# Attention scores of the first batch from plain fp32 products instead of products of rounded parts

## The chip, the cores and the metric

The kernel runs on one core of a Trainium2 chip. The metric is device time in microseconds (us), from the first to the last instruction and what lies around them. The core has five engines that run their own instruction streams in order: TensorE (PE; its weight loads are PEld), VectorE (DVE), ScalarE (ACT), GpSimd (POOL) and SyncE (SP, which here only issues transfers). They wait for each other by semaphores.

## The reference

Three stages follow one another. The first is attention over 4 batches of 8 heads, 576 positions, 64 numbers a head, with a threshold on the scores:

```
scores = scale * np.matmul(q, k.transpose(0, 1, 3, 2))
thresh = np.max(scores, axis=-1, keepdims=True) - tau
scores = np.where(scores >= thresh, scores, -1000000000.0)
scores = scores - np.max(scores, axis=-1, keepdims=True)
attn = np.exp(scores)
attn = attn / (np.sum(attn, axis=-1, keepdims=True) + 1e-09)
return np.matmul(attn, v).astype(np.float32)
```

The second is a dense layer pair (2304 tokens, 512 to 2048 to 512, a leaky rectifier between), the third a mixture of 8 experts with one expert a token. Both the threshold and the choice of the expert are decided by comparisons, so the products before them have to be close to fp32.

## The kernel before

**How precision is kept.** Most products run on numbers rounded to the type fp32r: the kernel splits an operand into a rounded part and a rounded residue and adds up the products of the parts. For scores, q and k of a pair of heads arrive twice: on partitions 0 to 63 and again on 64 to 127. The tile `qs` gets q rounded on all 128 partitions (ScalarE, L118 and L124), and then on partitions 64 to 127 the residue (`sub`, L110, on VectorE for pair 0 and on GpSimd for the others). The tiles `khh` and `kll` hold k times the scale, rounded (ScalarE, L116 and L122), and its residue (VectorE, `sub_k`, L113). One product of `qs` and `khh` over 128 partitions is then (q rounded + q residue) times k rounded, and one of `qs` and `kll` adds the same times k's residue.

**How the work is tiled.** A pair of heads (16 pairs, four a batch) has nine tiles of 128 score rows, numbered t = 0 to 8; n counts tiles over all pairs, i = n // 9 is the pair. Tile t = 4 holds the last 64 rows of the first head and the first 64 of the second. A tile's scores are two column halves of 288, each the sum of two products (t = 4: four), so four instructions at L152 (t = 4: eight). Then: the row's minimum of the negated scores (VectorE, L160), a bias (L164), the exponential (ScalarE, L169), the mask with its row sum (VectorE, L177), the split of the result in two 16-bit parts (ScalarE L196, GpSimd L197), a transposition by DMA (SP, L201), and five tiles later the products with v (TensorE, L216 or L222 to L224), scaled on the way out (L247 to L253). In the first batch, six tiles of nine take 25 products with v of 64 columns (L216), two take 15 and t = 4 takes 30.

**What sets the order.** A string is gone through once a tile, and each letter issues one step:

```
ORD = "QSMVaCRBbKOPcrTLoXd"
```

Q issues the scores of tile n + 2, S the split of n - 1, M the maximum of n + 1, V the products with v of n - 5, C one step of converting the dense layer's weights (ScalarE, VectorE, GpSimd; L382 to L390), B the bias of n + 1, K the mask of n, P a step of the next pair's preparation, T the transposition of n - 1, L the loads of pair i + 2, X the exponential of n + 1. The products with v are written beside the scores of tile n + 2 in the same PSUM tile, of which there are three. So the scores of n + 2 wait for the mask of n - 1, and the maximum of n + 2 waits for the scores and for the products with v that were issued right after them.

The preparation of a pair (`prep`) is a generator: each P takes one step of it (two in pair 0). The raw tiles of q, k and v have one buffer each, so a load waits until the pair before has been split. `LAT` says at which t the loads of k, q and v are issued. From tile 36 on other work (a class `Units`) is put between the steps; up to there only the weight conversion is.

Of the kernel before, what the change touches and what calls it, by code (L numbers as in the profile page):

```python
# [11 lines left out]
F32 = mybir.dt.float32  # L12
F32R = mybir.dt.float32r
# [3 lines left out]
AF = mybir.ActivationFunctionType  # L17
# [6 lines left out]
P = 128  # L24
B, H, S, D = 4, 8, 576, 64
HP = H // 2
# [15 lines left out]
def f(ap):  # L42
    return ap.bitcast(F32)


class Attention:
    def __init__(self, tc, ctx, qkt, vt, tau, xd):
        self.tc, self.qkt, self.vt, self.xd = tc, qkt, vt, xd
        nc = tc.nc
        cp = ctx.enter_context(tc.tile_pool(name="a_const", bufs=1))  # L50
        self.ld = ctx.enter_context(tc.tile_pool(name="a_ld", bufs=1))
        self.sp = ctx.enter_context(tc.tile_pool(name="a_split", bufs=2))
        self.ep = ctx.enter_context(tc.tile_pool(name="a_e", bufs=2))
        self.sm = ctx.enter_context(tc.tile_pool(name="a_sm", bufs=8))
        self.ptp = ctx.enter_context(tc.tile_pool(name="a_pt", bufs=PVL + 1))
        self.ps_s = ctx.enter_context(tc.tile_pool(name="a_ps_s", bufs=3, space=PSUM))
        tt = cp.tile([P, 1], F32, name="tau")
        nc.sync.dma_start(tt, tau.to_broadcast([P, 1]))
        self.c2 = cp.tile([P, 2], F32, name="c2")
        nc.vector.memset(self.c2, LNC)  # L60
        first = cp.tile([P, 1], F32, name="first")
        nc.scalar.activation(first, self.c2[:, 1:2], AF.Exp)
        keep = cp.tile([P, 1], F32, name="keep")
        nc.vector.tensor_scalar(keep, tt, 0.0, None, op0=ALU.is_ge)
        self.qsc = cp.tile([P, 1], F32, name="qsc")
        nc.vector.tensor_scalar(self.qsc, keep, -1.0 / float(D) ** 0.5, None, op0=ALU.mult)
        c1 = cp.tile([P, 1], F32, name="c1")
        nc.vector.tensor_scalar(c1, tt, 0.0, None, op0=ALU.max)
        nc.vector.tensor_scalar(keep, keep, -1.0, 1.0, op0=ALU.mult, op1=ALU.add)
        nc.vector.tensor_tensor(self.c2[:, 0:1], c1, keep, op=ALU.add)  # L70

        self.qs_b = [cp.tile([P, 2, 640], F32R, name=f"qs{i}") for i in range(2)]
        self.p_b = [cp.tile([P, 2, 640], F16, name=f"p{i}") for i in range(NP)]
        self.ss_b = [cp.tile([P, 9, 2], F32, name=f"ss{i}") for i in range(3)]
        self.rs_b = [cp.tile([P, 9], F32, name=f"rs{i}") for i in range(3)]
        for t in self.ss_b:
            nc.gpsimd.memset(t, 1e-9 * math.exp(LNC))
        for t in self.qs_b:
            nc.gpsimd.memset(f(t[:, 0, S:640]), 0.0)
        for t in self.p_b:  # L80
            nc.gpsimd.memset(t[:, :, S:640], 0.0)

    def load(self, k, i):

        nc = self.tc.nc
        b, hp = divmod(i, HP)
        r = self.raws.setdefault(i, {})
        if k < 2:
            r[k] = self.ld.tile([P, 2, S], F32, tag="qk"[k], name="raw_qk")
            if i:  # L90
                nc.sync.dma_start(r[k], self.qkt[b, hp][:, k])
        else:
            r[k] = self.ld.tile([P, 2, 5, D], F32, tag="v", name="raw_v")
            if i == 0:
                for h, j in ((0, 1), (0, 0), (1, 1), (1, 0)):
                    nc.sync.dma_start(r[j][:, h], self.qkt[b, hp][:, j, h])
            nc.sync.dma_start(r[k], self.vt[b, hp])

    def prep(self, i, eng):

        nc, sp, qsc = self.tc.nc, self.sp, self.qsc
        raw = self.raws.pop(i)
        qr, kr, vr = (raw[k] for k in range(3))
        qs = self.qs_b[i % 2]
        kk = [[sp.tile([P, S], F32R, tag=t, name=t, bufs=3) for t in ("khh", "kll")] for _ in range(2)]
        vs = sp.tile([P, 2, 5, 3, D], BF16, tag="vs", name="vs")
        vd = sp.tile([P, 2, 5, D], F32, tag="vd", name="vd", bufs=1)

        def sub(o, a, b, k):
            (eng if SUBS[k] == "p" else nc.vector).tensor_tensor(o, a, b, op=ALU.subtract)  # L110

        def sub_k(h):
            nc.vector.scalar_tensor_tensor(kk[h][1], kr[:, h], qsc, f(kk[h][0]), op0=ALU.mult, op1=ALU.subtract)  # L113

        self.pr[i] = qs, kk, vs
        nc.scalar.activation(kk[0][0], kr[:, 0], AF.Copy, scale=qsc)  # L116
        yield
        nc.scalar.activation(qs[:, 0, 0:S], qr[:, 0], AF.Copy)  # L118
        sub_k(0)
        yield  # L120
        sub(qs[D:P, 0, 0:S], qr[D:P, 0], f(qs[D:P, 0, 0:S]), 0)
        nc.scalar.activation(kk[1][0], kr[:, 1], AF.Copy, scale=qsc)  # L122
        yield
        nc.scalar.activation(qs[:, 1, 0:S], qr[:, 1], AF.Copy)  # L124
        sub_k(1)
        yield
        sub(qs[D:P, 1, 0:S], qr[D:P, 1], f(qs[D:P, 1, 0:S]), 1)
        yield
        nc.scalar.activation(vs[:, :, :, 0], vr, AF.Copy)
        yield  # L130
        sub(vd, vr, vs[:, :, :, 0], 2)
        yield
        nc.scalar.activation(vs[:, :, :, 1], vd, AF.Copy)
        yield
        sub(vs[:, :, :, 2], vd, vs[:, :, :, 1], 3)

    def score_mm(self, n):
        nc = self.tc.nc
# [124 lines left out]
    def run(self, npair):  # L263

        nc = self.tc.nc
# [14 lines left out]
        for n in range(nn + PVL + 2):  # L280
            i, t = divmod(n, 9)
            for w in ORD:
                if w == "a":
                    yield "start"
                elif w == "b":
                    yield "mid"
                elif w == "c":
                    yield "late"
                elif w == "C":
                    yield "conv"  # L290
                elif w == "d":
                    yield "tail"
                elif w == "P":
                    if t == 0 and i + 1 < npair:
                        g_prep = self.prep(i + 1, nc.gpsimd)
                        if i == 0:
                            g_prep = itertools.chain(g, [None] * 4, g_prep)
                    for _ in range(2 if i == 0 else 1):
                        next(g_prep, None)
                elif w == "S":  # L300
                    if 0 < n <= nn:
                        self.split(n - 1)
                elif w == "M":
                    if n + 1 < nn:
                        self.score_max(n + 1)
                elif w == "R":
                    if n <= nn:
                        self.sums(n - 1, 1)
                elif w == "O":
                    self.pv_out(1)  # L310
                elif w == "B":
                    if n + 1 < nn:
                        self.score_bias(n + 1)
                elif w == "Q":
                    if n + 2 < nn:
                        self.score_mm(n + 2)
                    else:
                        self.free = self.ps_s.tile([P, 2, 512], F32, tag="s", name="s")[:, 1, 320:320 + 2 * D]
                elif w == "V":
                    last, self.done = self.done, []  # L320
                    if 0 <= n - PVL < nn:
                        self.pv(n - PVL)
                elif w == "K":
                    if n < nn:
                        self.score_mask(n)
                elif w == "X":
                    if n + 1 < nn:
                        self.score_exp(n + 1)
                elif w == "T":
                    if 0 < n <= nn:  # L330
                        self.turn(n - 1)
                elif w == "o":
                    self.pv_out(0, last)
                elif w == "r":
                    if n < nn:
                        self.sums(n, 0)
                elif w == "L":
                    if n < 3:
                        self.load((1, 0, 2)[n], 1)
                    k = LAT[i > 0].find(str(t))  # L340
                    if k >= 0 and i + 2 < npair:
                        self.load((1, 0, 2)[k], i + 2)
            yield "end"


# [847 lines left out]
LAT = ["678", "457"]  # L1193
# [154 lines left out]
def body(tc, qkt, vt, tau, win, wout, mid, wg, wgt, mb, w1, w2, out):  # L1348
    nc = tc.nc
    with ExitStack() as top, tc.manual_schedule():  # L1350
# [12 lines left out]
        with ExitStack() as c1:  # L1363
            c0 = ExitStack()
            tp = c0.enter_context(tc.tile_pool(name="first", bufs=1, side="right"))
            at = Attention(tc, c1, qkt, vt, tau, xd)
            steps = at.run(B * HP)
            next(steps)
            cv = mo.convs(list(range(NF)), itertools.cycle(un.raws).__next__,
# [148 lines left out]
```

## Time and profile before

| | |
|---|---|
| three runs, us | 1058.48, 1061.03, 1061.22 (median 1061.03) |
| profiled execution, us | 1063.25, its span 1061.5 |
| mean granted clock of TensorE | 0.954 of full speed |
| busy over the span | TensorE 89%, VectorE 75%, ScalarE 56%, GpSimd 39% |

The page gives shares over the whole span; a stage is read from the views that can be cut to a stretch: busy time by stretch, groups of instructions by source line, waits, and the timeline. The clock column is the share of full speed that TensorE was granted: its levels are 1.2 GHz (0.5) and 2.4 GHz (1.0), so a mean between them says how much of a stretch was spent at which. In the first 28 us the column reads 1.00, while the score products start 0.24 us apart as they do at 1.2 GHz elsewhere; there the timeline is to be believed. The score tiles of the first batch are those between the first mask at 10.76 us and the 36th at about 113 us.

### The profile page before, as it was taken

Reading aid. Unit: us, or ns where it says so; the run is one execution under the profiler, and the core shown is the slowest. Engines: PE = TensorE matmul, PEld = TensorE weight load, DVE = VectorE, ACT = ScalarE, POOL = GpSimd, SP = SyncE. Lnnn points to the kernel's source line nnn. Section 1 sums busy time; section 2 is a strip of 40 time slices with the busy share of each in tenths; the row PEclk is TensorE's granted clock in tenths of the full one; section 3 lists DMA queues with packets and bytes.
Section 4 is the critical chain, followed back from the end, with each engine's and each line's share of the span. In section 5 each row is a group of like instructions: output and inputs, shape, how many; then the busy total and the mean of one; then the engine's idle time right before and its main releaser. Section 6 shows DMA issues by size and latency. Waiting matters only on the chain. (4 is left out here: it accounts for less than half of the span.)

```text
span 1061.5 us, 21618 instructions
## 1 busy us (share of the span) xinstructions
PE 944.1 (89%) x7593; PEld 841.5 (79%) x7593; DVE 790.8 (75%) x1975; ACT 597.7 (56%) x1234; POOL 415.0 (39%) x376
## 2 busy tenths in 40 slices
PE   4676679998999999788899999999989999999983
PEld 3666568888888999667788888989878999898962
DVE  7999988888888885887777777475558666655573
ACT  6677787888788875444222222323345555565473
POOL 3889887777778673332000000000102211121121
PEclk9879889999999999799999999999989999999997
DMA  8999999999999997542322321100555998665573
GB/s 216 197 223 222 232 243 228 211 218 254 210 196 242 236 181 144 177 143 84 112 61 60 60 41 41 41 21 1 120 180 153 341 300 289 229 242 169 171 253 118
DMA packets 278766, 182.03 MB, mean 171 GB/s; under 512 B 204450, under 2 KB 241446, under 8 KB 278632
## 3 DMA queue, kind: packets, MB, share of 16 engines
q1 hardware_dynamic: 270176, 165.25, 64.5%
q0 software_dynamic: 4736, 12.92, 3.6%
q10 hardware_dynamic: 3720, 2.22, 0.7%
q8 instruction: 65, 1.06, 0.5%
q14 instruction: 69, 0.57, 0.2%
HBM read 115.74 MB, written 18.22 MB: 126 GB/s over the span
## 5 line engine op out<-in xcount | busy, mean ns | idle before, releaser
L449 PE MATMUL y<-w,g 128*128 128x512 f32 x960 | 259.5, 406 | 0.0
L197 POOL TENSOR_TENSOR p<-p,p 128x576 f16<-128x576 f32 x144 | 193.1, 1342 | 86.9 <-ACT p L196 69.7
L449 PEld LDWEIGHTS y<-w,g 128*128 128x128 f32 x960 | 173.2, 193 | 29.6
L417 PE MATMUL h<-uxh,w 128*128 128x256 f32 x848 | 168.7, 295 | 17.4 <-POOL w L390 6.5
L417 PEld LDWEIGHTS h<-uxh,w 128*128 128x128 f32 x848 | 138.6, 195 | 31.0 <-DVE g L431 11.5
L152 PE MATMUL s<-khh,qs 128*128 128x288 f32 x320 | 107.2, 348 | 45.7 <-DVE p L177 23.0
L160 DVE TENSOR_REDUCE s<-s 128x1 f32<-128x576 f32 x144 | 109.3, 759 | 38.7 <-PE s L224 34.0
L429 ACT ACTIVATE g<-h 128x256 fp32r<-128x256 f32 x144 | 55.4, 385 | 129.3 <-DVE h L427 127.4
L417 PE MATMUL h<-uxl,w 128*128 128x256 f32 x424 | 122.3, 289 | 0.7 <-DVE uxl L408 0.7
L601 POOL DMA_INDIRECT idt<-ids,pi x18 | 18.7, 1040 | 264.2 <-DVE pi L598 196.4
L222 PE MATMUL s<-vs,pt 128*128 128x128 bf16 (+1 forms) x680 | 109.9, 229 | 13.6 <-DMA pt<-p 13.4
L177 DVE SCALAR_TENSOR_TENSOR p<-s,tb,e 128x576 f32<-128x576 f32 x144 | 117.0, 813 | 0.7 <-ACT e L169 0.6
L425 ACT ACTIVATE ct<-h 128x256 f32<-128x256 f32 x144 | 55.2, 383 | 109.9 <-PE h L417 102.7
L152 PEld LDWEIGHTS s<-khh,qs 128*128 128x128 f32 x320 | 67.8, 212 | 54.1 <-DVE p L177 15.5
L169 ACT ACTIVATE e<-s,tb 128x576 f32<-128x576 f32 x144 | 106.8, 741 | 4.9 <-DVE tb L164 4.9
L224 PE MATMUL s<-vs,pt 128*128 128x128 bf16 (+1 forms) x680 | 108.1, 226 | 0.0
L223 PE MATMUL s<-vs,pt 128*128 128x64 bf16 (+1 forms) x680 | 104.7, 198 | 0.0
L427 DVE SCALAR_TENSOR_TENSOR h<-h,ct 128x256 f32<-128x256 f32 x144 | 61.5, 427 | 54.5 <-ACT ct L425 53.8
L196 ACT ACTIVATE p<-p 128x576 f16<-128x576 f32 x144 | 99.2, 689 | 3.4 <-DVE p L177 2.1
L152 PE MATMUL s<-kll,qs 128*128 128x288 f32 x320 | 98.8, 322 | 0.0
L222 PEld LDWEIGHTS <-pt 128*128 128x128 f16 (+1 forms) x680 | 68.8, 104 | 26.4 <-DMA pt<-p 16.5
L417 PE MATMUL h<-exh,w 128*128 128x256 f32 (+1 forms) x448 | 85.8, 287 | 0.7 <-ACT exh L406 0.7
(233 smaller groups left out, 2270.2 us busy)
## 6 DMA issues: line engine op xcount, KB each, us to landing
cr<-w SPq DMA_DIRECT2D x36, 512.0 KB
raw_qk<-qkt SPq DMA_DIRECT2D x30, 576.0 KB
raw<-w SPq DMA_DIRECT2D x24, 512.0 KB
eraw<-w SPq DMA_DIRECT2D x18, 512.0 KB
cr<-w_in SPq DMA_DIRECT2D x16, 512.0 KB
cr<-w_out SPq DMA_DIRECT2D x16, 512.0 KB
ur<-xd SPq DMA_DIRECT2D x15, 512.0 KB
ur<-w SPq DMA_DIRECT2D x12, 512.0 KB
```

The lines of the kernel that those rows point to most:

```text
L152: nc.tensor.matmul(s[:, j, 0:288], qf[:, c0:c0 + P], x[:, j * 288:(j + 1) * 288], start=(k == 0), stop=(k == len(ops) - 1))
L160: v.tensor_reduce(self.mq[n], self.sq[n], axis=AX.XY, op=ALU.min)
L169: self.tc.nc.scalar.activation(e, self.sq[n], AF.Exp, bias=self.mq[n][:, 1:2], scale=-1.0)
L177: self.tc.nc.vector.scalar_tensor_tensor(p, self.sq.pop(n), self.mq.pop(n)[:, 0:1], self.eq.pop(n), op0=ALU.is_le, op1=ALU.mult, accum_out ...
L196: nc.scalar.activation(pp[:, 0, 0:S], p, AF.Copy)
L197: nc.gpsimd.tensor_tensor(pp[:, 1, 0:S], p, pp[:, 0, 0:S], op=ALU.subtract)
L222: nc.tensor.matmul(o[r0:r1, 0:2 * D], hi, v12, start=(c == 0), stop=False)
L223: nc.tensor.matmul(o[r0:r1, D:2 * D], hi, vs[:, h, c, 2], start=False, stop=False)
L224: nc.tensor.matmul(o[r0:r1, 0:2 * D], lo, v12, start=False, stop=(c == 4))
L417: nc.tensor.matmul(h, w[:, 0, a, s], b[:, c], start=(n == 0), stop=(n == 11))
L427: nc.vector.scalar_tensor_tensor(h, h, 0.01, a, op0=ALU.mult, op1=ALU.max)
L449: nc.tensor.matmul(y, a[:, s], w[:, 1, b], start=start and k == 0, stop=stop and k == 2)
```

## The change

For the four pairs of the first batch (i < HP) q and k are loaded once, on partitions 0 to 63. q goes to one of two new tiles `qa0` and `qa1` of its own and is used as it is; k is scaled by ScalarE into a `khh` tile seen as fp32. There are no residues of q and k. A tile's scores are one plain fp32 product for each column half (t = 4: two). The preparation of such a pair has seven steps instead of nine: v's four steps come two tiles earlier. The loads of pair 3 are issued at t = 4 (k) and 7 (q and v) of pair 1 instead of 4, 5 and 7. From pair 4 on everything is as it was; the old steps have moved into a function of their own, `prep_parts`.

```
@@ -44,7 +44,7 @@
 
 
 class Attention:
-    def __init__(self, tc, ctx, qkt, vt, tau, xd):
+    def __init__(self, tc, ctx, q0p, qkt, vt, tau, xd):
         self.tc, self.qkt, self.vt, self.xd = tc, qkt, vt, xd
         nc = tc.nc
         cp = ctx.enter_context(tc.tile_pool(name="a_const", bufs=1))
@@ -75,6 +75,9 @@
         self.rs_b = [cp.tile([P, 9], F32, name=f"rs{i}") for i in range(3)]
         for t in self.ss_b:
             nc.gpsimd.memset(t, 1e-9 * math.exp(LNC))
+        self.q0 = [q0p.tile([P, 2, 640], F32, name=f"qa{i}") for i in range(2)]
+        for t in self.q0:
+            nc.gpsimd.memset(t[0:D, 0, S:640], 0.0)
         for t in self.qs_b:
             nc.gpsimd.memset(f(t[:, 0, S:640]), 0.0)
         for t in self.p_b:
@@ -86,14 +89,19 @@
         b, hp = divmod(i, HP)
         r = self.raws.setdefault(i, {})
         if k < 2:
-            r[k] = self.ld.tile([P, 2, S], F32, tag="qk"[k], name="raw_qk")
+            if i < HP and k == 0:
+                r[k] = self.q0[i % 2][0:D, :, 0:S]
+            else:
+                r[k] = self.ld.tile([P, 2, S], F32, tag="qk"[k], name="raw_qk")
+                if i < HP:
+                    r[k] = r[k][0:D]
             if i:
-                nc.sync.dma_start(r[k], self.qkt[b, hp][:, k])
+                nc.sync.dma_start(r[k], self.qkt[b, hp][0:D if i < HP else P, k])
         else:
             r[k] = self.ld.tile([P, 2, 5, D], F32, tag="v", name="raw_v")
             if i == 0:
                 for h, j in ((0, 1), (0, 0), (1, 1), (1, 0)):
-                    nc.sync.dma_start(r[j][:, h], self.qkt[b, hp][:, j, h])
+                    nc.sync.dma_start(r[j][:, h], self.qkt[b, hp][0:D, j, h])
             nc.sync.dma_start(r[k], self.vt[b, hp])
 
     def prep(self, i, eng):
@@ -102,7 +110,11 @@
         raw = self.raws.pop(i)
         qr, kr, vr = (raw[k] for k in range(3))
         qs = self.qs_b[i % 2]
-        kk = [[sp.tile([P, S], F32R, tag=t, name=t, bufs=3) for t in ("khh", "kll")] for _ in range(2)]
+        if i < HP:
+            kk = [[f(sp.tile([P, S], F32R, tag="khh", name="khh", bufs=3))[0:D]] for _ in range(2)]
+            qs = self.q0[i % 2][0:D]
+        else:
+            kk = [[sp.tile([P, S], F32R, tag=t, name=t, bufs=3) for t in ("khh", "kll")] for _ in range(2)]
         vs = sp.tile([P, 2, 5, 3, D], BF16, tag="vs", name="vs")
         vd = sp.tile([P, 2, 5, D], F32, tag="vd", name="vd", bufs=1)
 
@@ -113,6 +125,24 @@
             nc.vector.scalar_tensor_tensor(kk[h][1], kr[:, h], qsc, f(kk[h][0]), op0=ALU.mult, op1=ALU.subtract)
 
         self.pr[i] = qs, kk, vs
+        if i < HP:
+            nc.scalar.activation(kk[0][0], kr[:, 0], AF.Copy, scale=qsc[0:D])
+            yield
+            yield
+            nc.scalar.activation(kk[1][0], kr[:, 1], AF.Copy, scale=qsc[0:D])
+            yield
+        else:
+            yield from self.prep_parts(qs, kk, qr, kr, sub, sub_k)
+        nc.scalar.activation(vs[:, :, :, 0], vr, AF.Copy)
+        yield
+        sub(vd, vr, vs[:, :, :, 0], 2)
+        yield
+        nc.scalar.activation(vs[:, :, :, 1], vd, AF.Copy)
+        yield
+        sub(vs[:, :, :, 2], vd, vs[:, :, :, 1], 3)
+
+    def prep_parts(self, qs, kk, qr, kr, sub, sub_k):
+        nc, qsc = self.tc.nc, self.qsc
...
@@ -337,9 +360,10 @@
                 elif w == "L":
                     if n < 3:
                         self.load((1, 0, 2)[n], 1)
-                    k = LAT[i > 0].find(str(t))
-                    if k >= 0 and i + 2 < npair:
-                        self.load((1, 0, 2)[k], i + 2)
+                    lat = "477" if 0 < i < HP - 2 else LAT[i > 0]
+                    for k in range(3):
+                        if lat[k] == str(t) and i + 2 < npair:
+                            self.load((1, 0, 2)[k], i + 2)
             yield "end"
 
 
@@ -1363,7 +1387,7 @@
         with ExitStack() as c1:
             c0 = ExitStack()
             tp = c0.enter_context(tc.tile_pool(name="first", bufs=1, side="right"))
-            at = Attention(tc, c1, qkt, vt, tau, xd)
+            at = Attention(tc, c1, tp, qkt, vt, tau, xd)
             steps = at.run(B * HP)
             next(steps)
             cv = mo.convs(list(range(NF)), itertools.cycle(un.raws).__next__,
```

In the program order of TensorE, at the start: before, the first two tiles of scores (`s_177`, `s_182`), from q's split tile `qs0` and the parts of k of the first head.

```order
L152 MATMUL s_177<-khh_166,qs0_131 128x288 [waits DVE_49]
L152 MATMUL s_177<-kll_167,qs0_131 128x288
L152 MATMUL s_177<-khh_166,qs0_131 128x288
L152 MATMUL s_177<-kll_167,qs0_131 128x288
L152 MATMUL s_182<-khh_166,qs0_131 128x288
L152 MATMUL s_182<-kll_167,qs0_131 128x288
L152 MATMUL s_182<-khh_166,qs0_131 128x288
L152 MATMUL s_182<-kll_167,qs0_131 128x288
```

Now the same place; `qa0` is q as loaded, `khh` the scaled k, and "x2" stands for two equal rows.

```order
L175 MATMUL s_175<-khh_169,qa0_148 128x288 [waits DMAHW2_49,Activation_49]
L175 MATMUL s_175<-khh_169,qa0_148 128x288
L175 MATMUL s_178<-khh_169,qa0_148 128x288 x2
L175 MATMUL s_186<-khh_169,qa0_148 128x288 x2
L175 MATMUL s_200<-khh_169,qa0_148 128x288 [waits DVE_49,PE_49]
L175 MATMUL s_200<-khh_169,qa0_148 128x288
```

Four products a tile have become two, and the first of them waits for a load (DMAHW) and ScalarE instead of VectorE. Later in the batch, VectorE's program order, from the mask of tile 5 (`p_351`) to the maximum of tile 8 (`s_362`), before:

```order
L177 SCALAR_TENSOR_TENSOR p_351,ss0_139<-s_270,tb_298,e_311 128x576 [waits Activation_49,Pool_49]
L113 SCALAR_TENSOR_TENSOR kll_303<-raw_qk_205,qsc_125,khh_302 128x576 [waits DMAHW0_49]
L187 TENSOR_REDUCE rs0_142<-ss0_139 128x3 [waits DVE_49]
L160 TENSOR_REDUCE s_313<-s_313 128x1 [waits PE_49]
L385 SCALAR_TENSOR_TENSOR yt1_92<-cr1_89,yt1_92 128x512
L189 RECIPROCAL rs0_142<-rs0_142 128x3 [waits DVE_49]
L164 TENSOR_TENSOR tb_387<-c2_119,s_313 128x2 [waits DVE_49]
L177 SCALAR_TENSOR_TENSOR p_389,ss0_139<-s_288,tb_349,e_360 128x576 [waits Activation_49,Pool_49]
L113 SCALAR_TENSOR_TENSOR kll_305<-raw_qk_205,qsc_125,khh_304 128x576
L160 TENSOR_REDUCE s_362<-s_362 128x1 [waits PE_49]
```

Now, from the mask of tile 5 (`p_326`) to the maximum of tile 8 (`s_335`); line numbers are those of the changed file, 23 or 24 higher.

```order
L200 SCALAR_TENSOR_TENSOR p_326,ss0_139<-s_252,tb_281,e_288 128x576 [waits Activation_49,Pool_49]
L210 TENSOR_REDUCE rs0_142<-ss0_139 128x3 [waits DVE_49]
L183 TENSOR_REDUCE s_290<-s_290 128x1 [waits PE_49]
L409 SCALAR_TENSOR_TENSOR yt1_92<-cr1_89,yt1_92 128x512
L212 RECIPROCAL rs0_142<-rs0_142 128x3 [waits DVE_49]
L187 TENSOR_TENSOR tb_358<-c2_119,s_290 128x2 [waits DVE_49]
L200 SCALAR_TENSOR_TENSOR p_360,ss0_139<-s_273,tb_324,e_333 128x576 [waits Activation_49,Pool_49]
L183 TENSOR_REDUCE s_335<-s_335 128x1 [waits PE_49]
```

The two residues of k (`kll`) behind the masks are gone; the steps of the weight conversion (`yt1`) and the sums (`rs0`) stand where they stood.

## Rows read from the trace of the kernel before

**Rows 1.** The page: busy time of the engines, and two of the 40 slices' rows.
```profile
PE 944.1 (89%) x7593; PEld 841.5 (79%) x7593; DVE 790.8 (75%) x1975; ACT 597.7 (56%) x1234; POOL 415.0 (39%) x376
...
PE   4676679998999999788899999999989999999983
...
DVE  7999988888888885887777777475558666655573
```

**Rows 2.** Busy time, clock and DMA by stretch; the line of columns is the second.
```profile
core 0: us, PE busy (x) PEld busy (x) DVE busy (x) ACT busy (x) POOL busy (x), PEclk, DMA share, GB/s
10.70:114.00 103.30, 69.28 (x849) 61.54 (x848) 99.15 (x215) 76.26 (x142) 83.81 (x71) 0.83 1.04 216
30.00:114.00 84.00, 57.73 (x780) 51.81 (x780) 79.95 (x174) 61.63 (x119) 72.16 (x64) 0.80 1.05 218
150.00:240.00 90.00, 83.27 (x897) 75.70 (x896) 77.09 (x211) 74.16 (x153) 68.55 (x60) 0.98 1.10 220
```

**Rows 3.** Groups by line, VectorE, 10.7 to 114 us: busy, mean ns, idle before.
```profile
L160 DVE TENSOR_REDUCE s<-s 128x1 f32<-128x576 f32 x35 | 26.4, 753 | 3.5 <-PE s L216 2.3 <-PE s L224 1.2
...
L113 DVE SCALAR_TENSOR_TENSOR kll<-raw_qk,qsc,khh 128x576 fp32r<-128x576 f32 x9 | 9.2, 1018 | 0.0
...
L110 DVE TENSOR_TENSOR qs<-raw_qk,qs 64x576 fp32r<-64x576 f32 x1 | 0.8, 755 | 0.0
```

**Rows 4.** Waits, 10.7 to 114 us: total us, times, longest.
```profile
PE s L152 <- DVE p L177: 21.9, 18, 2.9
...
PE s L222 <- DMA pt<-p: 0.8, 1, 0.8
```

**Rows 5.** Timeline, a cold tile: start, length, engine, line, [idle before].
```profile
59.70 0.80 DVE L177 SCALAR_TENSOR_TENSOR p<-s,tb,e 128x576 f32<-128x576 f32 x1
...
60.44 0.75 DVE L160 TENSOR_REDUCE s<-s 128x1 f32<-128x576 f32 x1
...
60.79 0.33 PEld L152 LDWEIGHTS s<-kll,qs 128*128 128x128 f32 x1
...
61.27 0.44 PE L152 MATMUL s<-khh,qs 128*128 128x288 f32 x1
...
61.51 0.44 PE L152 MATMUL s<-kll,qs 128*128 128x288 f32 x1
...
61.75 1.56 PE L216 MATMUL s<-vs,pt 128*128 128x64 bf16 x25
...
63.35 0.77 DVE L160 TENSOR_REDUCE s<-s 128x1 f32<-128x576 f32 x1 [1.22 <-PE s L216]
```

**Rows 6.** Timeline, TensorE in a tile at the high level.
```profile
81.25 0.29 PE L152 MATMUL s<-kll,qs 128*128 128x288 f32 x1
...
81.39 0.90 PE L216 MATMUL s<-vs,pt 128*128 128x64 bf16 x25
```

**Rows 7.** Groups by line, GpSimd, 10.7 to 114 us.
```profile
L110 POOL TENSOR_TENSOR qs<-raw_qk,qs 64x576 fp32r<-64x576 f32 x8 | 13.2, 1652 | 0.6
```

**Rows 8.** The line L385: ns min/median/max.
```profile
L385 DVE SCALAR_TENSOR_TENSOR yt<-cr,yt x32: 674/1641/1800, 16.6 to 493.1; 128x512 int32<-128x512 int32 x32
```

**Rows 9.** The line L554: ns min/median/max, first and last start in us.
```profile
L554 PEld LDWEIGHTS lp<-wg,ct x16: 188/192/192, 794.2 to 796.0; 128*128 128x128 f32 x16
L554 PE MATMUL lp<-wg,ct x16: 171/256/256, 794.4 to 796.0; 128*128 128x8 f32 x16
```

**Rows 10.** The line L586 likewise.
```profile
L586 PE MATMUL rp<-hot,ones x27: 166/166/167, 530.8 to 798.5; 128*128 128x8 bf16 x27
```

**Rows 11.** Timeline, the start.
```profile
5.03 0.77 ACT L116 ACTIVATE khh<-raw_qk,qsc 128x576 fp32r<-128x576 f32 x1 [2.71 <-DMA raw_qk<-qkt]
...
7.50 0.61 PE L152 MATMUL s<-khh,qs 128*128 128x288 f32 x1 [7.50 <-DVE qs L110]
...
8.86 0.77 DVE L160 TENSOR_REDUCE s<-s 128x1 f32<-128x576 f32 x1 [1.42 <-PE s L152]
...
10.76 0.82 DVE L177 SCALAR_TENSOR_TENSOR p<-s,tb,e 128x576 f32<-128x576 f32 x1
```

More of the change, by code (lines that the diff above doesn't have):

```diff
@@ L128, in prep @@
         yield
[L129 to L135, printed above, removed]
     def score_mm(self, n):
```

## The prediction

> **What bounds the kernel now.** I read the page first, for busy shares and slices, then the table by stretch, then the groups by line of the attention's first batch, its waits, and last a few microseconds of the timeline. Over the whole span TensorE is busiest (89%), but the slices show that this is a mean over unlike stages: in the first ten slices VectorE stands at 7 to 9 and TensorE at 4 to 7 [rows 1]. The change touches only the 36 score tiles of the first batch; their masking passes on VectorE run from 10.76 us to about 114. In that stretch of 103.30 us VectorE is busy 99.15, GpSimd 83.81, ScalarE 76.26 and TensorE 69.28 with a clock of 0.83 [rows 2]. So VectorE sets the pace: 103.3/35 = 2.95 us a tile from mask to mask, and all its idle time is 103.3 - 99.2 = 4.1 us, of which 3.5 stand before the row maximum L160 [rows 3], waiting for TensorE. The other side of the same fact: TensorE's scores wait 21.9 us for L177 [rows 4], which gives their PSUM buffer back. TensorE has slack there, and the question is how much of it the new products eat.
>
> TensorE's slack depends on its clock. A tile is four 288-column score products and, on six tiles of nine, 25 products with v. At the low level (1.2 GHz) scores start 0.24 us apart and the 25 take 1.56 [rows 5]; at 2.4 GHz 0.14 and 0.90 [rows 6]. So one tile costs 4 x 0.24 + 1.56 = 2.5 us at the low level (cold, below) and 4 x 0.14 + 0.90 = 1.45 at the high one (warm). The maximum waits for both: at 63.35 VectorE takes up work 1.22 us late, when the 25 of the cold tile end [rows 5]. From 30 to 114 us the clock is 0.80, that is 40% of the time at the low level (0.6 x 1 + 0.4 x 0.5); from 150 to 240, where TensorE is busy 83.27 of 90 us, it is 0.98 [rows 2].
>
> **What goes.** Of VectorE: eight residues of k (L113) and two of q (L110) for four pairs. One of each lies before the stretch, in the start. Inside it nine L113 run, 1018 ns each, two of them for pair 4, which stay; so seven go, 7.1 us, with one L110 of 0.755 [rows 3]. Records overlap: L177 is 0.80 long but the next maximum starts 0.74 after it [rows 5], a factor of 0.92. So VectorE is freed of 7.9 x 0.92 = 7.2 us. As it is the bound, all of this is on the path, unless something else is late.
> From ScalarE eight copies of q go and from GpSimd six subtractions of 1.65 us (of the eight in the stretch two are pair 4's) [rows 7]. Neither is the bound: nothing directly. VectorE's integer pass L385 takes between 674 and 1800 ns for one and the same shape [rows 8]; the trace doesn't say on what that depends. If it is GpSimd's work beside it, less of it could give about 1 us, and a denser schedule could take it back. I count zero, with 1 us to either side.
> Loads: q and k of pairs 0 to 3 come on 64 partitions, half the bytes; their issues stay as many. Pair 1's q no longer waits for pair 0's buffer, pair 3's q is issued two tiles later, behind a transposition, and waits for TensorE's last score of pair 1, which by then is one tile old. Queued behind it on SP are that tile's transposition, which TensorE needs five tiles later, and v. TensorE's waits for transpositions are small in this stretch as it is, 0.8 us [rows 4]. I count these at nothing; v of pairs 1 to 3 is split two tiles earlier than now, and if a load were late there, ScalarE would stand with its exponentials behind it, 1 to 2 us once.
>
> **What comes.** Two plain products take the place of four. No wide plain product is in the trace. The nearest row is the router's L554: plain fp32, 8 columns, 8 instructions, and 16 records, so two records an instruction, 256 ns each [rows 9]; 16-bit products of the same 8 columns last 166 [rows 10]. Bounds: if each record streams its columns as a rounded product does, an instruction costs 2 x 0.14 = 0.28 us and the scores cost TensorE what they cost now. If weight load and stream of each record stood one behind the other, it would be 2 x (0.192 + 0.24) = 0.86 with the weight load of L554 and a stream twice as long. I take 0.50: two records, each streaming twice 288 columns (4 x 0.125), because the 90 ns by which L554's records are longer speak for a second stream in each, and because successive weight loads in that row start 0.11 us apart (first to last 794.2 to 796.0) and so fit under such a stream.
> The Trainium skill has a rule on this: "FP8 and Floating Point Precision", section TensorE Precision Notes, says that true FP32 makes four passes through the array. The trace shows two records an instruction and not what is in one; by a count of records alone the sum would be that of the cheap product below, by the page that of the forecast.
>
> A tile's TensorE work becomes, warm, 4 x 0.25 + 0.90 = 1.9 us, and the tile with two heads (t = 4: twice the scores, and 30 products with v, at the pace of the 25 at least 1.1) 2.0 + 1.1 = 3.1 or more; cold, 8 x 0.24 + 1.56 = 3.5. VectorE's own pitch falls to (99.15 - 7.2)/35 = 2.63. Between the mask that frees a buffer and the maximum that needs it lie one pitch and a few small VectorE passes, about 2.9 us, less about 0.2 for the signals. So a warm tile is hidden, a warm t = 4 late by some 0.3 (four of them, the first at the start cold and late by 1: some 2.0), a cold one late by 0.7.
> How many are cold? Cold, TensorE would now be busy without a break, and the rows show it rising to 2.4 GHz where it is denser; warm, it would be busy 1.9 plus its tail of 0.3 in 2.7, about 80%, which lies between the 69% (clock 0.80) and the 93% (0.98) of the two stretches [rows 2]. Weighting the cold tiles as full I put the clock at 0.92, 16% cold: of 29 tiles after 28 us 4.6, x 0.7 = 3.3 us.
> **The start.** Now k arrives, 5.03, and scores begin at 7.50 behind copies and residues on two engines; the first maximum starts at 8.86, the first mask at 10.76 [rows 11]. With plain products only k's scaling, 0.77, is ahead: k's load at half the bytes perhaps 0.4 earlier, so scores at about 5.5. But TensorE is cold there: each tile takes 1.92 instead of 0.96. The mask stands behind two tiles and the second maximum: 5.5 + 3.84 + 0.35 + 0.95 = 10.6. Gain 0.1.
>
> **The sum**, against the profiled execution's 1063.25 (span 1061.5 and 1.75 around it): VectorE -7.2; waits for TensorE, now 4.1, then 3.3 + 2.0 = 5.3, so +1.2; start -0.1: -6.1. I take 0.8 off for waits of the denser schedule that I can't see: -5.3, so 1057.9. The profiled execution is 2.2 above the median of the three (1061.03); the predicted median is 1055.7. What follows the first batch keeps its order and its work per tile, and starts earlier by as much.
>
> **Rivals.**
> *Cheap product* (0.28): waits shrink to about 2, and the start gains the 1.9 us by which scores start earlier. -7.2 - 2.1 - 1.9 = -11.2: 1049.8. For it: the count of records. Against it: their length.
> *The clock stays up* once it has risen: the 3.3 us of cold tiles go: -8.6: 1052.4. For it: the stretch with 93%. Against it: clock 0.83 over the whole stretch although TensorE runs without a break in some tiles. The Trainium skill, "TensorE: Matmul & The Clock Gate", Part 1, has this as its rule: the throttled state is the default and activity releases it. The trace agrees in direction, 0.80 to 0.98 [rows 2].
> *The cover is gone half the time*: the clock is as low as now, 40% of 29 tiles cold, 11.6 x 0.7 = 8.1 us of waits in place of 3.3: -0.5, so 1060.5, no change. For it: the new products make a warm stretch shorter in time than the old ones made a cold one, and the gaps that let the clock fall stay.
> *Slower*: the second record's weight load isn't hidden, in any tile of the batch. At 0.86 a product a t = 4 tile takes 3.4 + 1.1 = 4.5 warm, late by 1.6 (6.5 us over four), a cold tile, whose weight load takes 0.33 [rows 5], 2 x 2 x (0.33 + 0.48) + 1.56 = 4.8, late by 2 (9 over 4.6), and the start loses 2 x 1.3: waits of about 18 and 1063.25 + 18 - 4.1 - 7.2 = 1070 profiled, 1067.7 as a median. It decides from about 0.65 a product, where the same reckoning gives waits of 11 = 7.2 + 4.1. For it: no row shows a wide plain product. Against it: the weight loads of L554 overlap.
> That the change doesn't do what it says is excluded by the order of the instructions shown above.
>
> **How the numbers follow.** Forecast 0.42 (own range 1053 to 1058.5), cheap product 0.10, clock stays up 0.15, cover gone 0.20, slower 0.13. What a measurement here can tell from no change is about 0.3%, 3.2 us: faster means under 1057.9. Faster: four fifths of 0.42, and 0.10 + 0.15, is 0.58. Same: most of the rest of the forecast, 0.07, and 0.19 of cover gone, 0.26. Slower 0.16: the slower case and edges. The range leaves out part of the cheap product below (0.07) and of the slower case above (0.12): 1049.5 to 1065.
>
> **What would show it.** Score products as two records each, starting 0.24 to 0.26 us apart at 2.4 GHz and 0.48 at 1.2 (wrong: 0.14, or over 0.32). VectorE busy about 92 us between first and last mask of the batch, masks 2.8 us apart. Its waits before the maximum about 5 us, behind products with v at the low clock. Clock over the batch's second half about 0.92. First mask at 10.6. The stretches after the batch as long as now; if they aren't, the sum was right only by chance.

## The result, and the profile after: slower by 1.5%

The changed kernel took 1076.27 us (median of four, 1067.93 to 1083.18) against 1061.12 (four, 1058.48 to 1063.83): a ratio of 1.0146, with a 95% interval of 1.0108 to 1.0185. The forecast was 1055.7, its range ended at 1065. The profiled execution took 1078.85, its span is 1076.6.

First the place. One number above has to be put right: the first batch's 36th mask is not at about 113 us, where the 35th is, but at 115.16. In the changed kernel it starts at 134.99. Timelines of VectorE, before and after:

```profile
115.16 0.80 DVE L177 SCALAR_TENSOR_TENSOR p<-s,tb,e 128x576 f32<-128x576 f32 x1
```
```profile
134.99 0.81 DVE L200 SCALAR_TENSOR_TENSOR p<-s,tb,e 128x576 f32<-128x576 f32 x1
```

So the batch alone is 19.8 us longer. From its 36th mask to the end the kernel before takes 1061.5 - 115.2 = 946.3 us, this one 941.6; over all kernels below that rest lies between 939.6 and 947.0 without a pattern, and nothing is made of it.

Busy time by stretch, before and after, from the first mask to behind the 36th [rows 2 has the same view], and for after two stretches of the inside:

```profile
10.70:116.00 105.30, 70.77 (x877) 62.83 (x876) 101.15 (x220) 77.92 (x145) 84.98 (x72) 0.84 1.03 217
```
```profile
30.00:60.00 30.00, 28.95 (x207) 20.06 (x204) 17.00 (x42) 12.06 (x24) 12.42 (x21) 1.00 0.66 143
60.00:90.00 30.00, 28.13 (x234) 19.86 (x235) 19.62 (x52) 17.23 (x33) 17.20 (x15) 1.00 0.74 147
10.70:135.80 125.10, 114.07 (x878) 79.50 (x876) 85.03 (x211) 73.43 (x137) 71.20 (x66) 0.89 0.82 170
```

VectorE (third of the busy times) works 16.1 us less and stands still 125.1 - 85.0 = 40.1 us instead of 4.2: 36 - 16 is the loss. TensorE (first) has become the bound: busy 28.95 us of the 30 from 30 to 60 us. The waits of after say for whom VectorE stands; [rows 3] had 3.5 us of this, and [rows 4] the reverse, TensorE waiting 21.9 us for VectorE:

```profile
DVE s L183 <- PE s L239: 17.0, 12, 2.9
DVE s L183 <- PE s L247: 14.7, 9, 2.4
...
PE s L175 <- DVE p L200: 10.3, 8, 2.7
ACT vs L136 <- PE s L239: 9.9, 2, 7.0
...
DVE p L200 <- ACT e L192: 6.3, 2, 4.2
ACT khh L132 <- PE s L175: 5.0, 2, 3.5
...
DVE s L183 <- PE s L175: 1.6, 2, 0.8
```

And the timeline of a tile shows why TensorE is late, beside [rows 5]:

```profile
61.63 2.26 PE L175 MATMUL s<-khh,qa 64*128 64x288 f32 x4 [2.68 <-DVE p L200]
...
63.81 1.52 PE L239 MATMUL s<-vs,pt 128*128 128x64 bf16 x25
...
65.26 2.28 PE L175 MATMUL s<-khh,qa 64*128 64x288 f32 x4
...
65.37 0.77 DVE L183 TENSOR_REDUCE s<-s 128x1 f32<-128x576 f32 x1 [1.27 <-PE s L239]
```

Scores take 2.18 us to the first product with v, the 25 products 1.45: a tile lasts 3.63 us, and that is its cost at 1.2 GHz (the 25 take 0.90 at 2.4). The clock column reads 1.00 from 30 to 90 us, as it did in the first 28 us of before: its first entry of this run lies at 92 us. The level is read better from the groups of 25, which are the same in all kernels here. Of the 21 in the batch, the timeline shows 13 of after at the low level (before: 7), and no high one ahead of 82 us (before: 30 us). Later, at 2.4 GHz, a tile with two heads:

```profile
83.35 2.20 PE L175 MATMUL s<-khh,qa 64*128 64x288 f32 x8
```

Eight records in 2.20, the last 0.40 long: 0.257 apart, two of them a product, 0.51 us.

### The profile page after: what moved, and what is told of

Read it like the earlier page. It is cut to its first block, busy times and chain, and to the rows that moved or that the text cites. A ratio compares the mean times of both kernels' runs of the same rounds, so it can differ in the third digit from the quotient of the medians.

```text
span 1076.6 us, 21585 instructions
## 1 busy us (share of the span) xinstructions
PE 986.8 (92%) x7593; PEld 856.7 (80%) x7593; DVE 773.7 (72%) x1965; ACT 592.5 (55%) x1226; POOL 399.7 (37%) x372
## 5 line engine op out<-in xcount | busy, mean ns | idle before, releaser
L220 POOL TENSOR_TENSOR p<-p,p 128x576 f16<-128x576 f32 x144 | 188.2, 1308 | 120.4 <-ACT p L219 103.1
L245 PE MATMUL s<-vs,pt 128*128 128x128 bf16 (+1 forms) x680 | 113.1, 233 | 9.3 <-DMA pt<-p 9.2
L247 PE MATMUL s<-vs,pt 128*128 128x128 bf16 (+1 forms) x680 | 111.8, 230 | 0.0
L246 PE MATMUL s<-vs,pt 128*128 128x64 bf16 (+1 forms) x680 | 108.1, 201 | 0.0
L175 PE MATMUL s<-khh,qa 64*128 64x288 f32 x160 | 77.3, 637 | 15.1 <-DVE p L200 9.6
L175 PE MATMUL s<-khh,qs 128*128 128x288 f32 x240 | 73.0, 320 | 11.6 <-DVE p L200 6.3
L441 PEld LDWEIGHTS h<-uxl,w 128*128 128x128 f32 x424 | 82.1, 194 | 1.1 <-DVE uxl L432 1.1
```

Of the source, the lines that this page charges most:

```text
L175: nc.tensor.matmul(s[:, j, 0:288], qf[:, c0:c0 + P], x[:, j * 288:(j + 1) * 288], start=(k == 0), stop=(k == len(ops) - 1))
L220: nc.gpsimd.tensor_tensor(pp[:, 1, 0:S], p, pp[:, 0, 0:S], op=ALU.subtract)
L245: nc.tensor.matmul(o[r0:r1, 0:2 * D], hi, v12, start=(c == 0), stop=False)
L246: nc.tensor.matmul(o[r0:r1, D:2 * D], hi, vs[:, h, c, 2], start=False, stop=False)
L247: nc.tensor.matmul(o[r0:r1, 0:2 * D], lo, v12, start=False, stop=(c == 4))
L441: nc.tensor.matmul(h, w[:, 0, a, s], b[:, c], start=(n == 0), stop=(n == 11))
```

## The experiments

Two theories of the low level were put against each other. *Rows*: it stays because the new products read 64 rows of the array instead of 128. *Plain*: because they are plain fp32. A third matter came up in the waits above: ScalarE, in two places, waits up to 7.0 us to write v's split (*the early v*). "Low" in the table counts those of the 21 groups of 25 products that last 1.3 us or more (about 1.5 with all 25 at 1.2 GHz, 0.9 with all at 2.4; up to three a run lie between the two); times are medians, the ratio is to the kernel before on the same chip.

| run | us | ratio, 95% interval | 36th mask | low |
|---|---|---|---|---|
| before (profiled run) | 1061.12 | | 115.16 | 7 |
| changed kernel | 1076.27 | 1.0146, 1.0108 to 1.0185 | 134.99 | 13 |
| e1_rows128 | 1060.55 | 0.9991, 0.9974 to 1.0008 | 112.01 | 1 |
| e2_before64 | 1064.03 | 1.0014, 0.9998 to 1.0030 | 118.06 | 19 |
| e3_cheap64 | 1056.12 | 0.9932, 0.9911 to 0.9954 | 108.21 | 18 |
| e4_rowpair | 1058.96 | 0.9965, 0.9946 to 0.9984 | 111.29 | 6 |
| e5_vlate | 1069.57 | 1.0099, 1.0068 to 1.0131 | 124.47 | 10 |
| e6_rows128_vlate | 1055.57 | 0.9959, 0.9943 to 0.9975 | 111.39 | 2 |
| e7_rowpair_vlate | 1053.67 | 0.9942, 0.9918 to 0.9966 | 109.20 | 3 |
| e8_rows128_zero (one run) | 1056.80 | | 110.95 | 2 |
| e9_zero64 | 1054.15 | 0.9954, 0.9935 to 0.9972 | 108.81 | 2 |
| e10_cheap64_vlate | 1047.18 | 0.9880, 0.9852 to 0.9909 | 106.06 | 17 |

**e1: plain products over 128 rows.** The edit, on the changed kernel (loads and tiles on all partitions likewise; `qsh` is half of `qsc`, so that the two halves of the rows add up to the same sums):

```
-            kk = [[f(sp.tile([P, S], F32R, tag="khh", name="khh", bufs=3))[0:D]] for _ in range(2)]
-            qs = self.q0[i % 2][0:D]
+            kk = [[f(sp.tile([P, S], F32R, tag="khh", name="khh", bufs=3))] for _ in range(2)]
+            qs = self.q0[i % 2]
...
-            nc.scalar.activation(kk[0][0], kr[:, 0], AF.Copy, scale=qsc[0:D])
...
+            nc.scalar.activation(kk[0][0], kr[:, 0], AF.Copy, scale=self.qsh)
```

> The changed kernel with its plain products over 128 rows of the array instead of 64: q and k of the first batch loaded on both halves of the partitions, k scaled by half as much, so the sums are the same. Streams and weight loads of TensorE stay as many and as long. In the changed kernel scores start at 1.2 GHz until 81 us although TensorE is busy 97% of 30 to 60 us. Theory rows (the low level stays because the plain products use half the array's rows): 2.4 GHz from about 30 us on, 36th mask at about 108 us instead of 133, time 1053 to 1058. Theory plain (plain fp32 products hold the level low, whatever their rows): 36th mask at 125 to 135 us, time 1066 to 1083 as the changed kernel.

Measured: 1060.55, and the level is high from the first group of 25 on, at 23 us, but for one group. The loss is gone, with as many records, as long:

```profile
59.82 0.89 PE L239 MATMUL s<-vs,pt 128*128 128x64 bf16 x25
...
61.64 1.21 PE L175 MATMUL s<-khh,qa 128*128 128x288 f32 x4 [0.93 <-DVE gsel L545]
```

*Rows* holds for the level. Not for the time: 112.0 and 1060.55 instead of 108 and 1053 to 1058, so something else takes up the relief.

**e2: the kernel before on 64 rows.**

```
-                nc.tensor.matmul(s[:, j, 0:288], qf[:, c0:c0 + P], x[:, j * 288:(j + 1) * 288],
+                r = slice(0, D if i < HP else P)
+                nc.tensor.matmul(s[:, j, 0:288], qf[r, c0:c0 + P], x[r, j * 288:(j + 1) * 288],
...
```

> The kernel before, with the first batch's four rounded products a tile reading only partitions 0 to 63 of q and k (q's residue, which lies on 64 to 127, is left out of the scores). Everything else, VectorE's and GpSimd's preparation too, stays. Theory rows: the clock from 30 to 114 us falls well under the 0.80 of before, to 0.5 to 0.65; a tile then costs TensorE 2.5 us at the low level, under VectorE's 2.9, so the time rises by 0 to 4 us only. Theory plain: clock 0.80 as before, time as before, 1061.

Measured: 1064.03, a change of 0.0 to 0.3%, and 19 of 21 groups low; the first high one comes at 117 us, behind pair 4's first products over 128 rows. So rounded products on 64 rows keep the level low too, and *plain* is out. It is cheap there, since a rounded tile at 1.2 GHz still fits under VectorE's pitch.

```profile
42.36 1.52 PE L217 MATMUL s<-vs,pt 128*128 128x64 bf16 x25
...
46.03 1.51 PE L217 MATMUL s<-vs,pt 128*128 128x64 bf16 x25
```

**e3: one rounded product, still on 64 rows.** On the changed kernel: `khh` stays of type fp32r, and ScalarE copies q rounded into `qs_b` in the two empty steps.

> The changed kernel with one rounded product in place of one plain one (q copied rounded by ScalarE, k scaled rounded; the residues of q and k are left out of the scores), still on 64 rows. A score tile costs TensorE two streams of 288 columns instead of eight. This asks what the relief of VectorE and of the start is worth when TensorE is no longer late. By the prediction's terms: 7.2 us of VectorE, 2 to 4 of waits and up to 1.9 of the start: 1061 - 9 to - 12, 1049 to 1052, 36th mask at 102 to 105 us. Both theories of the clock agree here, since at the low level a tile costs 2 x 0.24 + 1.56 = 2.0 us, under VectorE's 2.63. If it comes out at 1058 or more, the relief itself was mis-sized.

Measured: 1056.12, 36th mask at 108.2. A gain, short of the expected one by 4 to 7 us. Its waits show where they went: VectorE waits 4.6 us for ScalarE's exponentials, as in after.

**e4: two column halves on two halves of the array.** On the changed kernel, with q on all partitions and k's two column halves on the two halves of them:

```
...
+            for k, (c0, h) in enumerate(parts):
+                for j in range(2):
+                    r = slice(j * D, (j + 1) * D)
+                    nc.tensor.matmul(s[:, j, 0:288], qf[r, c0:c0 + P], kk[h][0][r],
+                                     start=(k == 0), stop=(k == len(parts) - 1))
```

> The changed kernel with the two column halves of a score tile on two halves of the array: q on both halves of the partitions, k's columns 0 to 287 on partitions 0 to 63 and 288 to 575 on 64 to 127, so each half's plain product reads its own 64 rows and the two alternate. Same products, same sums. If products on different rows run beside each other, a tile's scores cost TensorE half: 0.5 us at 2.4 GHz and about 1.1 at 1.2, and even at the low level 1.1 + 1.56 = 2.7 us is VectorE's pitch: 36th mask at 104 to 108 us, 1051 to 1056, under either theory of the clock. If they run one behind the other, it tells the theories apart as the 128-row run does only if the clock looks at rows over time; the time is then that of the changed kernel, 1066 to 1083.

Measured: 1058.96, 36th mask at 111.3, 3 us later than expected. The products do run beside each other: four records in 0.76 us, where e1 took 1.21. The Trainium skill, "TensorE: Matmul & The Clock Gate", Part 3, says that products on different row groups run at the same time; the trace agrees in that much. It also bears on a rival of *rows*, that the change to and fro between products over 64 and over 128 rows holds the level down: e4 changes as often as the changed kernel, but with both halves of the rows at work, and 6 of its groups are low instead of 13.

```profile
61.96 0.76 PE L184 MATMUL s<-khh,qa 64*128 64x288 f32 x4 [1.78 <-DVE p L214]
```

**e5: the changed kernel with v split later.** Two empty steps ahead of v's first copy:

```
             nc.scalar.activation(kk[1][0], kr[:, 1], AF.Copy, scale=qsc[0:D])
             yield
+            yield
+            yield
```

> The changed kernel with two empty steps ahead of v's split, so that v of pairs 1 to 3 is split at t = 5 as in the kernel before. In the changed kernel ScalarE's first copy of v waits 9.9 us in two places (7.0 the longest) for products with v of the pair before the last, whose tile it overwrites, and VectorE's mask waits 6.3 us for ScalarE. Theory wait (this is a second cause beside the clock): the waits go, 36th mask 4 to 7 us earlier than 135, time 5 us under the changed kernel's 1066 to 1083. Theory hidden (TensorE at 1.2 GHz sets the pace, ScalarE's stall lies beside it): time as the changed kernel.

Measured: 1069.57, below the changed kernel's median by 6.7 though within its spread (1067.93 to 1083.18); ScalarE's wait for products with v falls from 9.9 to 0.9 us, and no wait of VectorE for ScalarE is left in the list. By the ratios it gains 0.5%, 5 us, with intervals that overlap. It fits *wait*; but in its profiled run 10 groups are high instead of 7, so this pair alone doesn't part the wait from the level. The two hang together: at ScalarE's second stall in after, with its copy of v at 90.69 us, exponential and mask come late behind it, TensorE stands idle for 2.68 us, and its next products are back at 1.2 GHz until 112 us. In e5 the level stays high from 79 to 112 us, with the same products.

```profile
93.33 2.26 PE L175 MATMUL s<-khh,qa 64*128 64x288 f32 x4 [2.68 <-DVE p L200]
```

The first stall of after reads like this: ScalarE's copy of v comes after the products with v of pair 0's last tile, the exponential behind it, the mask behind that:

```profile
57.43 1.52 PE L239 MATMUL s<-vs,pt 128*128 128x64 bf16 x25
58.98 0.74 ACT L136 ACTIVATE vs<-raw_v 128x640 bf16<-128x640 f32 x1 [7.04 <-PE s L239]
...
59.82 0.73 ACT L192 ACTIVATE e<-s,tb 128x576 f32<-128x576 f32 x1
...
60.65 0.82 DVE L200 SCALAR_TENSOR_TENSOR p<-s,tb,e 128x576 f32<-128x576 f32 x1 [4.18 <-ACT e L192]
```

The tile for v's split has two buffers. Pair 2's takes pair 0's, whose last products with v are issued at t = 4 of pair 1; the changed kernel splits v at t = 3.

**e6: e1 and e5 together.**

> Both: plain products over 128 rows and v split two tiles later. The 128-row run took 1060.5 with its 36th mask at 112.0, the clock at 2.4 GHz in the whole batch, and waits of 6.1 us of ScalarE for products with v, 4.1 of VectorE for ScalarE. Theory wait: these go, 36th mask at 107 to 109, time 1056 to 1058. If it stays at 112, something else takes up VectorE's relief.

Measured: 1055.57. Chips differ by a microsecond or two, so kernels that ran on different chips are compared by their ratios to the kernel before: 0.9991 to 0.9959, 3.4 us less than e1, with intervals that overlap by 0.0001. The time is as expected, the 36th mask at 111.4 is not: in the profiled run TensorE waits 6.7 us for transpositions, which the prediction had at 0.8 [rows 4]:

```profile
PE s L247 <- DMA pt<-p: 6.7, 3, 3.6
```

**e7: e4 and e5 together.**

> The two column halves on two halves of the array and v split two tiles later. The run without the second edit took 1059.0, 36th mask at 111.3, waits of 7.3 us of ScalarE for products with v and 5.7 of VectorE for ScalarE. Theory wait: 36th mask at 106 to 108, time 1053 to 1056.

Measured: 1053.67; by the ratios 2.4 us less than e4, with intervals that overlap. TensorE waits 7.2 us for transpositions here.

**e8: the second half of the rows multiplies zeros.** e1 with k scaled by 0 on partitions 64 to 127.

> The 128-row run with k scaled to zero on partitions 64 to 127 (and fully on 0 to 63): the same sums, the same rows read, but the second half of the array multiplies zeros. If the level follows the rows that are addressed, the 25 products with v take 0.89 us in the whole batch, as in the 128-row run, 36th mask at 112. If it follows what the array does with the numbers, they take 1.5 until 80 us or so, 36th mask at 125 to 135.

Measured, one run: 1056.80, 2 of 21 groups low. So in these runs the level goes with the rows that are read, not with the numbers in them.

```profile
43.02 0.89 PE L240 MATMUL s<-vs,pt 128*128 128x64 bf16 x25
```

Rows are not the whole condition. In after the level rose twice with products over 64 rows, by 81 and by 112 us, each time behind a turn's 30 products with v over 128 rows (78.46 to 80.92 and 110.17 to 112.62 us); behind the first such turn (39.85 to 42.30), and in e2 behind all three, it stayed low. What lets it rise with these products is open.

**e9: 64-partition loads, zeros once, products over 128 rows, v later.**

```
+        self.kz = [q0p.tile([P, S], F32, name=f"kz{i}") for i in range(4)]
+        for t in self.kz:
+            nc.gpsimd.memset(t[D:P], 0.0)
+        for t in self.q0:
+            nc.vector.memset(t[D:P], 0.0)
...
+            kk = [[self.kz[2 * (i % 2) + h]] for h in range(2)]
+            qs = self.q0[i % 2]
```

> The changed kernel with q and k on 64 partitions as there (half the bytes), the other 64 partitions of q's two tiles and of four tiles for k set to zero once at the start, products over 128 rows, v split at t = 5, and two tiles for k more, so that no copy of k waits for scores. Against the 128-row run with v late (1055.6, where TensorE waited 6.7 us for transpositions by DMA) it moves 2.4 MB less in the first batch. If those waits came from the loads, 36th mask at 107 to 109 instead of 111.4 and 1051 to 1054; if they come from the denser transpositions themselves, 1054 to 1057 with the same waits.

Measured: 1054.15, faster than before by 0.28 to 0.65%; against e5, which differs in the rows and in two tiles for k, 1.0099 to 0.9954, 15 us. Waits for transpositions are 3.6 + 0.7 us instead of 6.7 + 0.6, the 36th mask is at 108.8, the time at the edge between the two answers (e6 1055.57, e9 1054.15, intervals overlap): that the loads make the transpositions late isn't settled. This is the change with its loads and its plain products kept, and the rows, the early v and the wait for k's tiles mended. Of the kernels that compute the whole, e7, e9 and e6 are fastest, and their intervals overlap. The stretch from the first mask to behind the 36th:

```profile
10.18:109.65 99.47, 73.24 (x877) 56.54 (x876) 90.64 (x212) 73.13 (x138) 72.56 (x66) 0.95 1.06 203
```

**e10: e3 with v later.**

> The run with one rounded product on 64 rows (residues of q and k left out of the scores) and v split at t = 5. It took 1056.1 with ScalarE's stall, VectorE waiting 4.6 us for ScalarE and 8.1 for TensorE. Asks for the prediction's largest term, VectorE's relief, with neither the stall nor late scores: 36th mask at 104 to 106, 1051 to 1053. If it stays at 108, the relief is taken up by something that no edit so far has touched.

Measured: 1047.18, better than expected by 4; 36th mask at 106.1 in the profiled execution, the longest of the four (1052.34). With scores this cheap the time is the lowest of all though 17 of 21 groups are low. By the ratios it is 5.5 us under e3, the intervals just apart (0.9909 and 0.9911): of the four pairs with and without the later v (5, 3.4, 2.4, 5.5 us) this is the clearest, with the level as good as the same (17 and 18 low).

## Why the prediction was wrong, step by step

- **The number of cold tiles** is the step that failed: "Cold, TensorE would now be busy without a break, and the rows show it rising to 2.4 GHz where it is denser", 4.6 tiles at 0.7, 3.3 us. TensorE was busy without a break (97% from 30 to 60 us) and stayed at 1.2 GHz until 81 us. The rows I drew the line through [rows 2] were all of products over 128 rows; the change halves the rows, and e1, e2 and e8 show that this alone keeps the level down for most of the batch. VectorE's waits for TensorE came to 17.0 + 14.7 + 1.6 = 33.3 us instead of 5.3. The rule in the Trainium skill, "TensorE: Matmul & The Clock Gate", Part 1, that activity releases the throttle, I had taken as speaking for the change; here busy time did not release it, and the measurement decides.
- **The price of a cold tile**, 0.7, was too low as well: 13 of 21, that is 18 of 29 tiles, would be 12.6 us at that price. Between 28 and 82 us VectorE's eleven waits for TensorE sum to 18.1 us, 1.6 each. With TensorE busy without a break a cold tile lasts 3.63 us, 1.0 more than VectorE's forecast pitch of 2.63, and longer turns find no slack. And the tile with two heads was misread: its scores and its products with v never meet in one turn of the order string, since a turn has the scores of n + 2 and the products of n - 5. One turn has its eight score records and 25 products, another has four records and its 30 products. Cold they take 5.58 us (45.97 to 51.55, below) and 4.67 (37.63 to 42.30).

```profile
45.97 4.20 PE L175 MATMUL s<-khh,qa 64*128 64x288 f32 x8
50.10 1.52 PE L239 MATMUL s<-vs,pt 128*128 128x64 bf16 x25
51.55 2.29 PE L175 MATMUL s<-khh,qa 64*128 64x288 f32 x4
```

- **The cost of a product** was right: 0.51 us at 2.4 GHz against 0.50, and at 1.2 GHz a tile of 3.63 against 3.5. So the rival *slower* came true in its sign, not by its mechanism: no weight load was in the way (records start 0.48 us apart at 1.2 GHz, beside weight loads of 0.33). The rival *the cover is gone* had the mechanism, with 40% of the tiles cold, a share taken from before, and 8.1 us of waits; it was 13 of 21 groups and 33.3 us.
- **v split two tiles earlier**: I asked only whether its load would be late, 1 to 2 us once. What it waits for is its buffer. In after VectorE lost 6.3 us to it, and the level fell behind the second stall (e5); the four pairs put its price at 2.4 to 5.5.
- **VectorE's relief**, 7.2 us, was mis-sized to the other side. In e9 VectorE is busy 90.64 against 101.15 in the batch, 10.5 less (groups sum to more, since records overlap): the residues of k go from 9.2 to 2.0 us, and the weight conversion's three passes from 29.0 to 24.9, with GpSimd's work in the stretch down from 84.98 to 72.56. I had counted zero with 1 us to either side; that GpSimd's work is the reason was not tried by itself. Groups of lines of e9, beside [rows 3, 8]:

```profile
L415 DVE SCALAR_TENSOR_TENSOR yt<-cr,yt 128x512 int32<-128x512 int32 x9 | 11.0, 1227 | 0.0
L417 DVE SCALAR_TENSOR_TENSOR yt<-yt,yt 128x512 int32<-128x512 int32 x8 | 7.3, 913 | 0.0
L413 DVE TENSOR_SCALAR yt<-cr 128x512 int32<-128x512 int32 x9 | 6.6, 736 | 0.0
...
L129 DVE SCALAR_TENSOR_TENSOR kll<-raw_qk,qsc,khh 128x576 fp32r<-128x576 f32 x2 | 2.0, 996 | 0.0
```

The groups of the kernel before for the same passes, from 10.7 to 116 us:

```profile
L385 DVE SCALAR_TENSOR_TENSOR yt<-cr,yt 128x512 int32<-128x512 int32 x9 | 11.1, 1231 | 0.0
L387 DVE SCALAR_TENSOR_TENSOR yt<-yt,yt 128x512 int32<-128x512 int32 x8 | 9.4, 1171 | 0.0
L113 DVE SCALAR_TENSOR_TENSOR kll<-raw_qk,qsc,khh 128x576 fp32r<-128x576 f32 x9 | 9.2, 1018 | 0.0
L383 DVE TENSOR_SCALAR yt<-cr 128x512 int32<-128x512 int32 x9 | 8.5, 943 | 0.0
```

- **The start**: first mask at 10.4 instead of 10.76, forecast 10.6: right, and for the reason given, scores that start at 5.2 and run cold.
- **Loads and transpositions at nothing**: no worse in after, where the pace is slow; at e6's pace TensorE waits 6.7 us for them.
- **Carried to the end**: not to be read from one execution each, with a rest that varies by 7 us.

With the level and the early v mended, e9 comes out near the forecast, in part by luck: it gains 10.5 of VectorE's work where 7.2 was forecast, its standstill grows by 4.7, from 4.15 to 99.47 - 90.64 = 8.83, where 1.2 was forecast, and the first mask comes 0.5 earlier. Its 36th mask is 6.35 earlier, and by the ratio it is 4.9 us faster (3.0 to 6.9). The forecast was -5.3: two terms were off by over 3 us each and made up for each other.

## What to carry to other kernels

A change that halves the rows of TensorE's products can cost more than the time of the products: look at what else runs on TensorE in that stretch and reckon it at the lower level, all of it, unless a row shows that level rising with products of that shape. Rows of zeros that fill the array up again cost little here (e9). When a step of a prepared pipeline is moved to an earlier turn, look first at who still reads the buffer that it writes, and only then at whether its input has come. And a clock column that reads 1.00 is to be checked against the length of a group of instructions that occurs everywhere.

## What the runs showed of the hardware that was not expected

- With score products over 64 rows between products with v over 128, TensorE stayed at 1.2 GHz while it was busy 28.95 of 30 us. With 128 rows, half of them zeros, it stood at 2.4 GHz from 24 us (e8) and 29 us on (e9), but for two groups of 25 and one, and was busy less (73.24 of 99.47 us in e9).
- A product over 64 rows costs no less than one over 128: records at 2.4 GHz are at least 402 ns long on 64 rows in after and 406 on 128 in e1, and a tile's four take 1.21 us in both.
- A plain fp32 product of 288 columns is two records 0.257 us apart at 2.4 GHz and 0.48 at 1.2. On two halves of the array four such records ended after 0.76 us instead of 1.21.
